# Rotary attention and a dense mixture of experts in one kernel: the softmax sums' constant, the spread's engine, and the order of work in the boundary between the two parts

## The chip, the core and the metric

The kernel runs on one core of one Trainium2 chip. A core has five engines that run their own instruction streams and wait for each other through semaphores: TensorE (PE in the rows, with its weight loads as PEld), VectorE (DVE), ScalarE (ACT), GpSimd (POOL) and SyncE (SP, which here only issues DMAs). The metric is device microseconds of one execution; where several runs are shown, their median. Line numbers (L361) are those of the kernel before.

## The reference

```python
# q, k, v: (2 batches, 8 heads, 576 positions, 64); w1: (4, 512, 1024); w2: (4, 1024, 512)
q_rot, k_rot = rotate(q), rotate(k)                      # rotary embedding on halves of 32
scores = np.matmul(q_rot, k_rot.transpose(0, 1, 3, 2)) / np.sqrt(D)
scores = scores - np.max(scores, axis=-1, keepdims=True)
attn = np.exp(scores)
attn = attn / (np.sum(attn, axis=-1, keepdims=True) + 1e-09)
x = np.matmul(attn, v)                                   # then heads are joined: (1152 tokens, 512)
p = domain_probs / (domain_probs.sum(-1, keepdims=True) + 1e-09)
for e in range(4):
    out += p[:, e:e + 1] * (np.maximum(x @ w1[e], 0.0) @ w2[e])
```

All four experts work on all tokens. Everything is float32.

## The kernel before, in words

**Numbers.** A float32 product of large matrices is made of three matmuls on rounded operands: each operand x is split into a high part (a copy rounded by the engine that writes it) and a low part (x minus the high part). For the weights `split` does that (L139 on ScalarE for `wh`, L146 on POOL for `wl`); for the tokens the pairs write `xH` and `xL`.

**Stages.** Tokens come in two chunks: chunk 0 is the first 512 positions of batch 0, chunk 1 the rest. A *pair* is two heads of one batch; there are four pairs in each batch. First the four pairs of batch 0 run alone (up to about 100 us). Then the experts of chunk 0 start (`start_experts`, at the agenda's time `end`), and the four pairs of batch 1 run between their matmuls: the boundary of which this document speaks is where this begins. About 350 us into the span the experts of chunk 1 begin.

**A pair.** Its keys and queries are loaded, rotated (on POOL), transposed on TensorE (`tpk`, `tpq`), and kept as `kT`, `qT` and `qTt` (the last 64 positions). In batch 1 `turn_whole` makes five transposes and `keep_whole` copies the high halves on ScalarE (L293) and writes the low ones on VectorE (L295); `swap` then exchanges the halves of the keys by two DMAs on SP (`k2T`). A pair has nine units: scores on TensorE (`sc`), the maximum on VectorE (`mx`), the exponential on ScalarE (`e`), which also adds up its rows into one column of `total`; transposes of e (`pp`), rounded as `pt` and `ptX`, and values (`x`). After the ninth unit `inverse` adds 1e-9 to the nine sums and takes their reciprocal (both on VectorE, in place), and `spread` copies eight of them out to a 128x512 tile (`rep`), which TensorE turns so that `divide` can multiply by it. `tail_rows` does that for the ninth.

**Experts.** For chunk 0, expert e has eight steps of the first layer (`ph`, f = 0 to 7, twelve matmuls of 512 columns each, then `hH` on ScalarE and `hL` on VectorE) and eight of the second (`po`), whose results VectorE adds into `acc`.

**Weights.** They come in blocks of 128x1024, one SP DMA each into one of two raw buffers (`wr`); a block's raw buffer is free when POOL has written its `wl`. `wts.next` issues the load of the next block and splits the one loaded before; there are five places for split blocks.

**What sets the order.** Each engine runs its instructions in the order in which the program issues them. The order comes from an agenda: `plan.at(t, f)` puts a piece of code at a time t in units of a pair's unit or an expert's step, and `plan.run` calls them by t. `ALONE` and `BESIDE` hold the times of a unit's pieces, `NEXT_TURNS` those at which a pair of batch 1 is turned (the first entry for the first pair, whose times are relative to the start of its scores, the second for the others). `later` puts a piece into a queue of jobs, of which two are done at each expert's step.

Of the kernel before, what the change touches and what calls it, by code (L numbers as in the profile page):

```python
# [14 lines left out]
F32 = mybir.dt.float32  # L15
F32R = mybir.dt.float32r
AF = mybir.ActivationFunctionType
ALU = mybir.AluOpType
AX = mybir.AxisListType
# [31 lines left out]
]  # L51
FIRST_TURNS = dict(q0=(1.327, 1.45), q1=(2.3, 2.5), q_tails=(-0.037, 0.16), swap=1.4)
NEXT_TURNS = [
    dict(k=(-0.75, -0.74), q=(0.6, 0.601), swap=(0.07,)),
    dict(k=(0.03, 0.056), q=(0.975, 1.004), swap=(0.07,)),
]


# [1 line left out]
def kernel(  # L60
# [36 lines left out]
    def f32(ap):  # L97
        return ap.bitcast(F32)
# [50 lines left out]
    class Pair:  # L149
# [196 lines left out]
        def scores(self, u):  # L346
            nm = f"{self.nm}_{u}"
            if u == 0:
                self.total = self.pool.tile([P, U], F32, tag="total", name=f"total{self.nm}")
            a = 0 if u % 2 else ST  # L350
            kT, kT2 = (self.tr[x][:, :, a : a + S] for x in ("k", "k2"))
            if u < TAIL:
                j, r = divmod(u, NR)
                qs = self.tr["q"][:, j, r * P : (r + 1) * P]
                terms = [(qs, kT[:, j, :]), (qs, kT2[:, j, :])]
            else:
                terms = [(self.qTt[:, j * P : (j + 1) * P], kk[:, j, :]) for j in range(2) for kk in (kT, kT2)]
            sc = banks["s"].tile([P, 2, 512], F32, f"sc{nm}")
            for n, (lhsT, rhs) in enumerate(terms):
                for i in range(2):  # L360
                    nc.tensor.matmul(  # L361
                        sc[:, i, 0:HALF],
                        lhsT=lhsT,
                        rhs=rhs[:, i * HALF : (i + 1) * HALF],
                        start=(n == 0),
                        stop=(n == len(terms) - 1),
                    )
            self.sc[u] = sc
# [8 lines left out]
        def exp(self, u):  # L377

            if u % 2 == 0:
                self.e2 = apool.tile([P, 2 * S], F32, tag="e", name=f"e{self.nm}_{u}", bufs=NE)  # L380
            a = u % 2 * S
            e = self.e2[:, a : a + S]
            nc.scalar.activation(  # L383
                out=e.rearrange("p (i c) -> p i c", i=2),
                in_=self.sc.pop(u)[:, :, 0:HALF],
                func=AF.Exp,
                bias=self.mx.pop(u),
                accum_out=self.total[:, u : u + 1],
            )
            self.e[u] = e[:, ST:] if u % 2 else e[:, 0:SM]  # L390
            if self.b == 0 or u == TAIL:
                self.ex[u] = self.e2[:, SM + u % 2 * ST :][:, 0:ST]
            elif u % 2:
                self.ex[u] = self.e2[:, SM : SM + P]
# [88 lines left out]
            )  # L483

        def inverse(self):
            nc.vector.tensor_scalar_add(self.total, self.total, 1e-9)
            nc.vector.reciprocal(out=self.total, in_=self.total)

        def spread(self):
            self.rep = apool.tile([P, NR, 2, D], F32, tag="rep", name=f"rep{self.nm}")  # L490
            by_row = self.total[:, 0:TAIL].rearrange("p (j r) -> p r j", j=2)
            nc.vector.tensor_copy(self.rep, by_row.unsqueeze(3).to_broadcast([P, NR, 2, D]))

        def rows(self):

# [5 lines left out]

        def tail_rows(self):
            self.prt = xb[1][:, 0:P] if banks["x"].n > 1 else xb[0][:, 3 * P : 4 * P]
            nc.tensor.transpose(self.prt, self.total[:, TAIL:].to_broadcast([P, P]), ident)

        def keep_tail_rows(self):
            if self.whole is None:
# [75 lines left out]
    class Weights:  # L583


        def __init__(self):
            self.order = [
                (c, e, which, fb)
                for c in range(NCHUNK)
                for e in range(E)  # L590
                for which in ((0, 2, 1) if c and not e else (0, 1))
                for fb in range(NF // FB)
            ]
            self.sums, self.lows = {}, collections.deque()
            self.raw, self.got = {}, {}
            self.loaded = self.done = 0

        def load(self):
# [13 lines left out]
            self.raw[key] = raw, f  # L612
            self.loaded += 1

        def split(self):
            if self.done == len(self.order):
                return
            key = self.order[self.done]
# [6 lines left out]
                return  # L625
            wh = wpool.tile([P, FB * DM], F32R, tag="h", name="wh%d_%d_%d_%d" % key, bufs=NRING)
            wl = wpool.tile([P, FB * DM], F32R, tag="l", name="wl%d_%d_%d_%d" % key, bufs=NRING)
            split(nc.scalar, nc.gpsimd, raw, wh, wl)
            self.got[key] = [x.rearrange("p (a f) -> p a f", f=f) for x in (wh, wl)]

        def finish(self):
# [20 lines left out]
            else:  # L652
                self.first_sums = lambda: split(nc.scalar, nc.gpsimd, x, sh, sl)

        def next(self):
            self.load()
            self.split()

    class Moe:

# [17 lines left out]
        def expert(self, e):  # L678
# [7 lines left out]
            for f in range(NF):  # L686
# [9 lines left out]
                        op0=ALU.max, op1=ALU.subtract,  # L696
                    )
                hh.append((tH, tL))
                if f % FB == FB - 1:
                    wts.next()  # L700
                yield
            po = [self.pp.tile([P, 512], F32, tag="m", name=f"po{c}_{e}_{t}") for t in range(n // P)]
# [313 lines left out]
    def pools(name, **kw):  # L1016
# [14 lines left out]
    first = [  # L1031
        Pair(0, hp, (evens, odds)[hp % 2], dst(0, hp, 0, SM), dst(1, hp, SM, S)) for hp in range(NP)
    ]
    qTt = [x.tile([P, 2 * P], F32R, name="qTt") for x in (evens, odds)]
    for x in (*qTt, tail_keys):
        nc.gpsimd.memset(f32(x), 0.0)
# [163 lines left out]
        plan.at(end + last - NF + 0.2 + 0.6 * i, quarter_step)  # L1200
    for i in range(6):
        plan.at(end + last - 1.3 + 0.1 * i, quarter_step)
    for t in (-1, 1.5, 5.3):
        plan.at(end + t, later(wts.next))
    plan.run()
    attn.close()
# [57 lines left out]
```

## Time and profile before

| | |
|---|---|
| runs | 568.74, 568.53, 567.66 us; median 568.53 us |
| the profiled execution | 567.32 us, span from first to last instruction 565.5 us |
| granted TensorE clock in it | 1.000 of full speed |
| TensorE busy | 537.2 us (95%) |
| VectorE, ScalarE, POOL busy | 334.8 us (59%), 288.0 us (51%), 326.5 us (58%) |

The rows are read as follows. In a timeline, each row has the start in us from the span's first instruction, the duration, the engine, the line, the operation, the tiles it writes and reads, their shapes, a count of merged instructions, and in brackets how long the engine was idle before it and which instruction ended the wait. Matmuls overlap, so that two that follow each other start closer together than a duration. The chain of waits follows the last instruction of a stretch back through what released it.

### The profile page before, as it was taken

To read this page: it belongs to the slowest core of one execution; us is meant where nothing else is said; L and a number is where in the kernel's file an instruction comes from. 1 tells how busy PE (TensorE), PEld (TensorE's weight loads), DVE (VectorE), ACT (ScalarE), POOL (GpSimd) and SP (SyncE) were. 2 spreads that over 40 slices of the span, in tenths; PEclk is the share of its full clock that TensorE was granted. 3 is DMA by queue.
4 is the path that set the end of the run, shared out by engine and by line. 5 is a ranking of instruction groups with operands and counts; after the bars stand their busy time and mean duration, and the time that the engine had idled before them with its cause. 6 is when DMAs were issued, how large, how long until landed. Compare 5 with 4: busy or idle time off the path is not lost.

```text
span 565.5 us, 8634 instructions
## 1 busy us (share of the span) xinstructions
PE 537.2 (95%) x3189; PEld 468.5 (83%) x3189; DVE 334.8 (59%) x617; ACT 288.0 (51%) x593; POOL 326.5 (58%) x241
## 2 busy tenths in 40 slices
PE   4898998989999999999999999999999999999996
PEld 3787787778877888788878888988898899889985
DVE  5589888354375435644365436894676576747602
ACT  5688888565545554655446553453344234325300
POOL 7999955459615752476344389558554664565400
PEclk9999999999999999999999999999999999999999
DMA  5245033244216221531242123622232213223102
GB/s 153 68 127 131 20 71 99 71 144 136 74 41 184 75 75 38 147 135 54 75 125 88 45 74 117 217 79 62 87 110 77 76 39 115 80 66 113 37 1 93
DMA packets 48732, 51.17 MB, mean 90 GB/s; under 512 B 15538, under 2 KB 38322, under 8 KB 48690
## 3 DMA queue, kind: packets, MB, share of 16 engines
q1 hardware_dynamic: 47890, 49.87, 29.3%
q10 hardware_dynamic: 800, 0.75, 0.5%
q8 instruction: 25, 0.41, 0.3%
q14 instruction: 17, 0.14, 0.1%
HBM read 43.34 MB, written 2.36 MB: 81 GB/s over the span
## 4 chain that ended last, share of the span: by engine, by line
PE 69%; DVE 11%; ACT 9%; POOL 5%; issue 3%; DMA 2%; SPq 1%; ACTq 0%; DVEq 0%; POOLq 0%
PE po L969 6%; PE po L970 6%; PE po L968 6%; PE sc L361 5%; PE p L880 5%; PE p L882 5%; PE p L881 5%; PE ph L734 4%; PE ph L735 4%; PE ph L733 4%; PE po L710 4%; PE po L708 4%; PE po L709 3%; PE pp L401 3%; ACT e L383 3%
## 5 line engine op out<-in xcount | busy, mean ns | idle before, releaser
L146 POOL TENSOR_TENSOR wl<-wr,wh 128x1024 fp32r<-128x1024 f32 x64 | 154.3, 2415 | 142.6 <-ACT wh L139 142.6
L139 ACT ACTIVATE wh<-wr 128x1024 fp32r<-128x1024 f32 x64 | 67.2, 1052 | 25.0 <-issue 11.9
L372 DVE TENSOR_REDUCE mx<-sc 128x1 f32<-128x576 f32 x72 | 54.2, 753 | 33.4 <-PE sc L361 32.6
L146 POOL TENSOR_TENSOR sl<-sf,sh 128x1024 fp32r<-128x1024 f32 x16 | 38.5, 2407 | 43.2 <-ACT sh L139 43.2
L970 PE MATMUL po<-wh,hL 128*128 128x512 f32 x160 | 62.3, 389 | 0.0
L969 PE MATMUL po<-wl,hH 128*128 128x512 f32 x160 | 62.3, 389 | 0.0
L968 PE MATMUL po<-wh,hH 128*128 128x512 f32 x160 | 62.3, 389 | 0.0
L383 ACT ACTIVATE e<-sc,mx 128x576 f32<-128x576 f32 x72 | 53.3, 741 | 17.4 <-DVE mx L372 16.5
L708 PE MATMUL po<-wh,hH 128*128 128x512 f32 x128 | 51.5, 403 | 0.0
L733 PE MATMUL ph<-xH,wh 128*128 128x512 f32 x128 | 51.1, 400 | 0.3 <-DVE acc L743 0.3
L420 DVE TENSOR_TENSOR pt<-pp,pt 128x512 fp32r<-128x512 f32 x64 | 43.9, 687 | 12.6 <-ACT pt L416 11.9
L734 PE MATMUL ph<-xL,wh 128*128 128x512 f32 x128 | 50.2, 392 | 0.6 <-POOL xL L524 0.6
L416 ACT ACTIVATE pt<-pp 128x512 fp32r<-128x512 f32 x64 | 38.1, 596 | 24.1 <-PE x L470 17.4
L710 PE MATMUL po<-wh,hL 128*128 128x512 f32 x128 | 50.3, 393 | 0.0
L735 PE MATMUL ph<-xH,wl 128*128 128x512 f32 x128 | 50.2, 392 | 0.0
L709 PE MATMUL po<-wl,hH 128*128 128x512 f32 x128 | 50.0, 391 | 0.0
L401 PE MATMUL pp<-ident,e 128*128 128x128 f32 x288 | 45.4, 281 | 3.9 <-ACT e L383 2.2
L694 DVE SCALAR_TENSOR_TENSOR hL<-ph,hH 128x512 fp32r<-128x512 f32 x32 | 22.2, 692 | 42.9 <-ACT hH L693 42.8
L920 ACT ACTIVATE hH<-p 128x320 fp32r<-128x320 f32 x64 | 26.1, 435 | 38.4 <-DVE p L911 38.4
L139 ACT ACTIVATE sh<-sf 128x1024 fp32r<-128x1024 f32 x16 | 16.9, 1059 | 51.4 <-DVE sf L644 51.4
L401 PEld LDWEIGHTS pp<-ident,e 128*128 128x128 f32 x288 | 34.5, 144 | 10.4 <-ACT e L383 4.2
L644 DVE TENSOR_TENSOR sf<-wr 128x256 f32<-128x256 f32 x30 | 32.7, 1126 | 17.4 <-DMA wr<-in_moe_w_dram 17.4
(212 smaller groups left out, 1359.2 us busy)
## 6 DMA issues: line engine op xcount, KB each, us to landing
wr<-in_moe_w_dram SPq DMA_DIRECT2D x68, 512.0 KB, 3.5
k2T<-kT SPq DMA_DIRECT2D x14, 320.0 KB, 4.5
rawv<-in_v_dram SPq DMA_DIRECT2D x16, 128.0 KB, 3.4
out_dram<-acc SPq DMA_DIRECT2D x8, 256.0 KB, 2.8
rawk<-in_k_dram SPq DMA_DIRECT2D x7, 256.0 KB, 3.9
rawq<-in_q_dram SPq DMA_DIRECT2D x7, 256.0 KB, 3.0
rawv<-in_v_dram SPq DMA_DIRECT2D x16, 32.0 KB, 2.9
tabs<-in_rope_dram ACTq DMA_DIRECT2D x1, 320.0 KB, 3.4
```

What stands on the lines that cost most here:

```text
L139: nc.scalar.activation(out=hi, in_=src, func=AF.Copy)
L146: eng_l.tensor_tensor(out=lo, in0=src, in1=f32(hi), op=ALU.subtract)
L383: nc.scalar.activation(out=e.rearrange("p (i c) -> p i c", i=2), in_=self.sc.pop(u)[:, :, 0:HALF], func=AF.Exp, bias=self.mx.pop(u), accum ...
L401: nc.tensor.transpose(pp[:, c * P : (c + 1) * P], self.e[u][:, c * P : (c + 1) * P], ident)
L708: nc.tensor.matmul(po[t], lhsT=sH, rhs=wH, start=(f == 0), stop=False)
L710: nc.tensor.matmul(po[t], lhsT=sL, rhs=wH, start=False, stop=(f == NF - 1))
L733: nc.tensor.matmul(o, lhsT=wH[:, kt], rhs=xh, start=(kt == 0), stop=False)
L734: nc.tensor.matmul(o, lhsT=wH[:, kt], rhs=xl, start=False, stop=False)
L735: nc.tensor.matmul(o, lhsT=wL[:, kt], rhs=xh, start=False, stop=(kt == KT1 - 1))
L968: nc.tensor.matmul(po[t], lhsT=sH, rhs=wH, start=(f == 0), stop=False)
L969: nc.tensor.matmul(po[t], lhsT=sH, rhs=wL, start=False, stop=False)
L970: nc.tensor.matmul(po[t], lhsT=sL, rhs=wH, start=False, stop=(f == NF - 1))
```

## The change

Five things are changed.

1. The nine sums of a pair have a second column beside them, set once to 1e-9 (two tiles, one for the even pairs and batch 1, one for the odd pairs of batch 0). `inverse` adds the two columns by a tensor_reduce into a new tile `inv`, and takes the reciprocal there. Before, it was a tensor_scalar addition in place.
2. In batch 1, `spread` is an activation on ScalarE and no longer a copy on VectorE.
3. The third and fourth weight blocks of the first expert are no longer split by a job at `end - 1` and in step f = 1, but at `end - 5.5` and `end - 0.1`; their low parts on POOL are issued at `end - 0.15` and `end - 0.09`.
4. The first pair of batch 1 has its keys turned before `end` (and the exchange of halves issued there), its queries about half a unit earlier.
5. For the other pairs of batch 1 the queries are turned 0.3 units earlier.

```diff
 NEXT_TURNS = [
-    dict(k=(-0.75, -0.74), q=(0.6, 0.601), swap=(0.07,)),
-    dict(k=(0.03, 0.056), q=(0.975, 1.004), swap=(0.07,)),
+    dict(k=(-1.2, -1.19), q=(0.0, 0.001), swap=(-1.1,)),
+    dict(k=(0.03, 0.056), q=(0.7, 0.701), swap=(0.07,)),
 ]
...
             if u == 0:
-                self.total = self.pool.tile([P, U], F32, tag="total", name=f"total{self.nm}")
+                self.total = totals[self.pool is odds]
...
-                accum_out=self.total[:, u : u + 1],
+                accum_out=self.total[:, u, 0:1],
...
         def inverse(self):
-            nc.vector.tensor_scalar_add(self.total, self.total, 1e-9)
-            nc.vector.reciprocal(out=self.total, in_=self.total)
+            self.inv = apool.tile([P, U], F32, tag="inv", name=f"inv{self.nm}", bufs=2)
+            nc.vector.tensor_reduce(out=self.inv, in_=self.total, op=ALU.add, axis=AX.X)
+            nc.vector.reciprocal(out=self.inv, in_=self.inv)
 
         def spread(self):
             self.rep = apool.tile([P, NR, 2, D], F32, tag="rep", name=f"rep{self.nm}")
-            by_row = self.total[:, 0:TAIL].rearrange("p (j r) -> p r j", j=2)
-            nc.vector.tensor_copy(self.rep, by_row.unsqueeze(3).to_broadcast([P, NR, 2, D]))
+            by_row = self.inv[:, 0:TAIL].rearrange("p (j r) -> p r j", j=2).unsqueeze(3).to_broadcast([P, NR, 2, D])
+            if self.b:
+                nc.scalar.activation(out=self.rep, in_=by_row, func=AF.Copy)
+            else:
+                nc.vector.tensor_copy(self.rep, by_row)
...
-            split(nc.scalar, nc.gpsimd, raw, wh, wl)
+            nc.scalar.activation(out=wh, in_=raw, func=AF.Copy)
+            low = lambda: nc.gpsimd.tensor_tensor(out=wl, in0=raw, in1=f32(wh), op=ALU.subtract)
+            if defer:
+                self.deferred.append(low)
+            else:
+                low()
...
+        def finish_split(self):
+            self.deferred.pop(0)()
...
-                if f % FB == FB - 1:
+                if f % FB == FB - 1 and (e or f >= FB):
                     wts.next()
...
+    totals = [x.tile([P, U, 2], F32, name="total") for x in (evens, odds)]
+    for x in totals:
+        nc.gpsimd.memset(x[:, :, 1:2], 1e-9)
...
-    for t in (-1, 1.5, 5.3):
+    for t, u in ((-5.5, -0.15), (-0.1, -0.09)):
+        plan.at(end + t, lambda: wts.next(True))
+        plan.at(end + u, wts.finish_split)
+    for t in (1.5, 5.3):
         plan.at(end + t, later(wts.next))
```

What this does to the order is seen in three places. The first is ScalarE in the boundary, before (`wh_0_0_2` and `wh_0_0_3` are the third and fourth weight blocks' high parts, `xH` the last pair's tokens, `kT` the next pair's keys, `hH_0_0` and `hH_0_1` the first two steps of the experts):

```order
L476 ACTIVATE tmp_3_3_1463<-x_114 64x256
L546 ACTIVATE xH_74<-xt_3_1448 128x64
L521 ACTIVATE xH_73<-xf_3_1309 128x512
L693 ACTIVATE hH_0_0_1519<-ph_0_0_0_1506 128x512
L139 ACTIVATE wh_0_0_2_1525<-wr_0_0_2_1260 128x1024
L293 ACTIVATE kT_0_1535<-tpk_0_1529 64x512 x2
L293 ACTIVATE kT_0_1535<-tpk_0_1529 64x2x64 x2
L693 ACTIVATE hH_0_1_1557<-ph_0_1_0_1544 128x512
L139 ACTIVATE wh_0_0_3_1563<-wr_0_0_3_1523 128x1024
```

The same place in the changed kernel, whose line numbers are its own:

```order
L476 ACTIVATE tmp_3_3_1467<-x_114 64x256
L632 ACTIVATE wh_0_0_2_1472<-wr_0_0_2_1263 128x1024
L550 ACTIVATE xH_74<-xt_3_1452 128x64
L525 ACTIVATE xH_73<-xf_3_1312 128x512
L632 ACTIVATE wh_0_0_3_1500<-wr_0_0_3_1470 128x1024
L293 ACTIVATE kT_0_1510<-tpk_0_1503 64x512 x2
L293 ACTIVATE kT_0_1510<-tpk_0_1503 64x2x64 x2
L705 ACTIVATE hH_0_0_1550<-ph_0_0_0_1537 128x512
L705 ACTIVATE hH_0_1_1570<-ph_0_1_0_1557 128x512
```

The third block's rounding has moved in front of both xH, the fourth's in front of kT, and kT in front of the first hH. POOL's order is unchanged but for the two memsets at the start.

The second place is TensorE there: the end of the first step's twelve matmuls and the keys' transposes behind them, before (`xL_75` in the second row is the low part of the last pair's tokens where its chunk is read):

```order
L733 MATMUL ph_0_0_0_1506<-xH_73,wh_0_0_0_1247 128x512
L734 MATMUL ph_0_0_0_1506<-xL_75,wh_0_0_0_1247 128x512
L735 MATMUL ph_0_0_0_1506<-xH_73,wl_0_0_0_1248 128x512
L271 MATMUL tpk_0_1529<-ident,rotk_0_873 128x128 x5
L733 MATMUL ph_0_1_0_1544<-xH_73,wh_0_0_0_1247 128x512
```

In the changed kernel, the end of the attention of batch 0 and the start of the first step:

```order
L502 MATMUL pr_3_1475<-ident,rep_3_1465 128x128 x4
L535 MATMUL x_113<-at_3_8_1435,rawv_3_1067 64x64 x8
L535 MATMUL x_113<-tail_keys,rawv_3_1067 64x64 x2
L271 MATMUL tpk_0_1503<-ident,rotk_0_876 128x128 x5
L745 MATMUL ph_0_0_0_1537<-xH_73,wh_0_0_0_1250 128x512
L746 MATMUL ph_0_0_0_1537<-xL_75,wh_0_0_0_1250 128x512
```

The five transposes stand in front of the twelve matmuls and no longer behind them. The queries' transposes likewise stand behind the second step and no longer behind the third.

The third place is VectorE where the first pair of batch 1 ends, before:

```order
L486 TENSOR_SCALAR total_0_1648<-total_0_1648 128x9
L487 RECIPROCAL total_0_1648<-total_0_1648 128x9
L442 TENSOR_TENSOR ptX_0_6_1992<-x_113,ptX_0_6_1992 64x128 x2
L492 COPY rep_0_2076<-total_0_1648 128x512
L694 SCALAR_TENSOR_TENSOR hL_1_0_2092<-ph_1_0_0_2078,hH_1_0_2091 128x512
```

and in the changed kernel:

```order
L487 TENSOR_REDUCE inv_0_2072<-total 128x9
L488 RECIPROCAL inv_0_2072<-inv_0_2072 128x9
L442 TENSOR_TENSOR ptX_0_6_1995<-x_113,ptX_0_6_1995 64x128 x2
L706 SCALAR_TENSOR_TENSOR hL_1_0_2096<-ph_1_0_0_2082,hH_1_0_2095 128x512
L295 SCALAR_TENSOR_TENSOR kT_1_2105<-tpk_1_2099,kT_1_2105 64x512 x2
```

The copy has left VectorE; on ScalarE it stands between ptX and that hH.

## Rows read from the trace of the kernel before

**Rows 1.** The page, busy time and share of the span, TensorE and its weight loads.
```profile
PE 537.2 (95%) x3189; PEld 468.5 (83%) x3189; DVE 334.8 (59%) x617; ACT 288.0 (51%) x593; POOL 326.5 (58%) x241
```

**Rows 2.** Timeline, TensorE: instructions behind a stop, from 100 us on.
```profile
103.31 0.50 PE L734 MATMUL ph<-xL,wh 128*128 128x512 f32 x1 [0.64 <-POOL xL L524]
...
116.72 0.50 PE L361 MATMUL sc<-kT,qT 128*128 128x288 f32 x2 [0.61 <-DVE qTt L295]
...
121.30 0.66 PE L401 MATMUL pp<-ident,e 128*128 128x128 f32 x4 [1.08 <-ACT e L383]
...
165.50 0.39 PE L469 MATMUL x<-pt,vs 128*128 128x256 f32 x1 [1.13 <-DVE ptX L442]
...
226.26 0.50 PE L733 MATMUL ph<-xH,wh 128*128 128x512 f32 x1 [0.32 <-DVE acc L743]
...
373.18 0.42 PE L880 MATMUL p<-tH,sh 128*128 128x320 f32 x1 [0.56 <-DVE hL L922]
```

**Rows 3.** Chain of waits in the boundary: start, us on the chain, what.
```profile
104.05 0.55 PE tpk L271 x5
...
109.07 2.42 POOL wl L146
...
111.50 5.80 DMA wr<-in_moe_w_dram
...
117.39 1.06 ACT wh L139
118.45 0.49 ACT hH L693
...
119.66 0.68 DVE mx L372
```

**Rows 4.** Timeline, ScalarE in the boundary.
```profile
99.11 0.38 ACT L476 ACTIVATE tmp<-x 64x256 f32<-64x256 f32 x1 [1.48 <-PE x L472]
101.13 0.26 ACT L546 ACTIVATE xH<-xt 128x64 fp32r<-128x64 f32 x1 [1.64 <-DVE xt L541]
101.30 0.62 ACT L521 ACTIVATE xH<-xf 128x512 fp32r<-128x512 f32 x1
...
105.53 1.75 ACT L293 ACTIVATE kT<-tpk 64x512 fp32r<-64x512 f32 x4
```

**Rows 5.** Timeline, POOL in the boundary.
```profile
101.99 1.27 POOL L524 TENSOR_TENSOR xL<-xf,xH 128x512 fp32r<-128x512 f32 x1 [0.20 <-ACT xH L521]
105.71 2.40 POOL L146 TENSOR_TENSOR wl<-wr,wh 128x1024 fp32r<-128x1024 f32 x1 [2.45 <-ACT wh L139]
```

**Rows 6.** The page, DMA issues: queue, count, size, median us to landing.
```profile
wr<-in_moe_w_dram SPq DMA_DIRECT2D x68, 512.0 KB, 3.5
k2T<-kT SPq DMA_DIRECT2D x14, 320.0 KB, 4.5
```

**Rows 7.** Line L486 by itself: shortest, median and longest duration in ns.
```profile
L486 DVE TENSOR_SCALAR total<-total x8: 172/460/1735, 33.2 to 338.0; 128x9 f32<-128x9 f32 x8
```

**Rows 8.** Timelines of VectorE and POOL, at 47 and at 162 us.
```profile
47.40 0.17 DVE L129 TENSOR_REDUCE ptot<-probs 128x9 f32<-128x36 f32 x1
...
162.84 1.74 DVE L486 TENSOR_SCALAR total<-total 128x9 f32<-128x9 f32 x1 [0.64 <-ACT e L383]
...
46.23 1.41 POOL L199 TENSOR_TENSOR t1k<-rawk,tabs 128x576 f32<-128x576 f32 x1
...
162.16 2.38 POOL L146 TENSOR_TENSOR wl<-wr,wh 128x1024 fp32r<-128x1024 f32 x1 [6.68 <-ACT wh L139]
```

**Rows 9.** Timeline, ScalarE: two hH with the waits before them.
```profile
163.86 0.60 ACT L693 ACTIVATE hH<-ph 128x512 fp32r<-128x512 f32 x1 [0.61 <-PE ph L735]
...
320.76 0.60 ACT L693 ACTIVATE hH<-ph 128x512 fp32r<-128x512 f32 x1 [1.57 <-PE ph L735]
```

**Rows 10.** Timeline, VectorE before the seam at 373 us.
```profile
347.75 1.28 DVE L550 TENSOR_TENSOR xL<-whole,xH 128x64 fp32r<-128x64 f32 x1 [0.32 <-ACT xH L546]
348.95 1.37 DVE L524 TENSOR_TENSOR xL<-whole,xH 128x512 fp32r<-128x512 f32 x1
```

More of the change, by code (lines that the diff above doesn't have):

```diff
@@ L503, in tail_rows @@
             self.prt = xb[1][:, 0:P] if banks["x"].n > 1 else xb[0][:, 3 * P : 4 * P]
-            nc.tensor.transpose(self.prt, self.total[:, TAIL:].to_broadcast([P, P]), ident)
+            nc.tensor.transpose(self.prt, self.inv[:, TAIL:].to_broadcast([P, P]), ident)
         def keep_tail_rows(self):
@@ L594, in __init__ @@
             self.sums, self.lows = {}, collections.deque()
-            self.raw, self.got = {}, {}
+            self.raw, self.got, self.deferred = {}, {}, []
             self.loaded = self.done = 0
@@ L613, in load, with split @@
             self.loaded += 1
-        def split(self):
+        def split(self, defer=False):
             if self.done == len(self.order):
@@ L653, in sum, with next @@
                 self.first_sums = lambda: split(nc.scalar, nc.gpsimd, x, sh, sl)
-        def next(self):
+        def next(self, defer=False):
             self.load()
-            self.split()
+            self.split(defer)
+        def finish_split(self):
+            self.deferred.pop(0)()
     class Moe:
```

## The prediction

> **What bounds the kernel now.** I read the page's busy shares first: TensorE is busy 95% of the span, and no other engine comes near [rows 1]. Where one engine is that full, time can only be won where it stands still, so the next view was the timeline of TensorE, read for the idle time in brackets. From the end of the first attention stage (100 us) on there are few stops, and six of them matter here [rows 2]. Three lie in the boundary between attention and the experts: 0.64 us for the last low part of the tokens (POOL xL), 0.61 us for the turned queries of the second batch's first pair (DVE qTt), 1.08 us for the first exponential (ACT e). One of 1.13 us lies where that pair ends (DVE ptX), one of 0.32 us at 226 us, one of 0.56 us in the seam to the second half of the tokens (373 us). Then I followed the chain of waits back from the largest of the boundary [rows 3]: the e waits for mx (DVE, 119.66), that for an hL and an hH, those for a weight rounding on ScalarE (117.39), that for a load of 5.8 us issued at 111.50, and the load for its buffer, which POOL's wl of 109.07 gives back. So the 1.08 us comes from weight rounding that starts too late, while in the same boundary ScalarE sits idle for 1.48 us before 99.11 and 1.64 us before 101.13 [rows 4].
>
> **The change, part by part.**
>
> *Two blocks rounded earlier.* ScalarE's row for the third block's high half now stands behind tmp, which ends at 99.11 + 0.38 = 99.49. One rounding takes 1.06 us [rows 3], so it ends at 100.55. The next instruction, xH from xt, cannot start before 101.13, since VectorE's xt releases it [rows 4]: 0.58 us to spare, cost nothing. If that cover were gone, each microsecond would be one on the path, since POOL's xL and the waiting matmul follow. The fourth block's rounding stands behind the xH that ends at 101.30 + 0.62 = 101.92, and ends at 102.98. On POOL both low halves stay behind the xL that ends at 103.26 [rows 5], so the matmul that waits for xL isn't touched; they run at 103.3 to 105.7 and 105.7 to 108.1, where they now start at 105.71 [rows 5] and 109.07 [rows 3]. The load that waits for the second is issued at 108.1, 3.4 us before its 111.50. With its present 5.8 us it lands at 113.9, and its rounding ends at 115.0.
>
> *Keys and queries turned earlier.* The five transposes of the keys take 0.55 us of TensorE, now after the xL wait [rows 3]; moved in front of the first ph they fill that wait: 0.64 becomes 0.09, gain 0.55 us. ScalarE copies kT at 102.98 instead of 105.53 [rows 4]; VectorE's half, and SP's exchange of key halves behind it (4.5 us to land [rows 6]), move with it by some 2.5 us. The queries are transposed one block of twelve matmuls earlier and on ScalarE no longer stand behind a rounding that waits for a load. Two hH later (about 107.6) ScalarE and then VectorE need about 1.75 us each, as for kT [rows 4], so qTt is ready near 111. TensorE reaches the score at 116.72 - 0.61 - 0.55 = 115.56: the 0.61 us is gone.
>
> *The first exponential.* From 115.56 on ScalarE isn't held by the load (115.0), so it waits for TensorE's fifth ph alone. From that hH (118.45) to the waiting matmul (121.30) are 2.85 us [rows 2, 3], which makes 118.4. TensorE comes there after a score and a block of matmuls, 121.30 - 1.08 - 116.72 = 3.5 us after 115.56, at 119.06. So 0.65 us to spare, and the 1.08 us is gone too. Boundary: 0.55 + 0.61 + 1.08 = 2.24 us.
>
> *The constant by tensor_reduce.* The eight tensor_scalar of nine columns take between 172 and 1735 ns [rows 7]. The longest, at 162.84, ends with POOL's wl that began at 162.16 and took 2.38 [rows 8]: it was held by POOL. A tensor_reduce to nine columns from SBUF took 0.17 us at 47.40 while POOL was in an instruction of 1.41 us that began at 46.23 [rows 8], so it isn't held. Then the reciprocal and ptX come 1.74 - 0.17 = 1.57 us earlier, more than the 1.13 us that TensorE waits for ptX [rows 2]; gain 1.13 us. The other three of the second batch end ahead of waits for other engines: nothing. For the first four the bounds are 0 and four times the median's excess, 4 x (460 - 172) ns = 1.2 us [rows 7]; the chain there goes through scores and exponentials and not through L486, so I take 0.
> The Trainium skill (SBUF — State Buffer, section Who interferes with whom) says the same as these rows for this chip, that copy and tensor_scalar can be shut out by GpSimd for a whole instruction and tensor_reduce never; another page (VectorE: DVE Perf Modes, Rules for kernel authors) speaks against the change, calling tensor_reduce the slowest VectorE operation. By that the eight might cost a little more than tensor_scalar does alone; the rows show 0.17 against 172 ns, so the sum stays.
>
> *The spread on ScalarE.* Four activations of 128x512; the nearest row of that size from SBUF is 0.62 us [rows 4]. In the first pair it stands in front of an hH that now waits 0.61 us for TensorE [rows 9]; in the other three the instruction behind it waits longer than that. Its input is ready when ptX ends on ScalarE. So nothing on the path; without that cover 4 x 0.62 = 2.5 us at the most.
>
> *The later turn.* For the third and later pairs the queries' transposes move forward; by the order only the third pair's pass a ph, and there they stand in front of the matmul that waits 0.32 us for acc [rows 2]: 0.55 us of work fills it, gain 0.32 us. The two memsets at the start lie in POOL's wait for the first load.
>
> Sum: 2.24 + 1.13 + 0.32 = 3.69, say 3.7 us. The profiled execution took 567.32 us (span 565.5 us), so it would take 563.6 us. That execution is 1.2 us under the median of the three runs shown, 568.53 us; taken from the median the sum gives 564.8 us, which I predict.
>
> **Rivals.**
> 1. *The load stays the bound.* Two weight loads and the key exchange now start between 105.7 and 108.1, closer together than before, and the 5.8 us was already longer than a weight load's usual landing of 3.5 us [rows 6]. If it lands after 115.2 (7 us), each further microsecond stays a stop. For it: the crowding. Against it: 1.2 us of room. With the whole 1.08 us left: 565.9 us.
> 2. *The reduce is held by POOL as well.* One row only speaks against it, and its overlap lasted just to POOL's end. Then the 1.13 us stays: 566.0 us.
> 3. *The lead is given back at the seam of 373 us.* There TensorE waits for VectorE [rows 2], behind a chain through POOL and ScalarE that starts with the hH of 320.76 [rows 9]. If that chain ran by loads, it would not come earlier, the 0.56 us would grow, and nothing much is left: 568 us. Against it: that hH waits for TensorE itself, so the chain should move along.
> 4. *More in the first stage.* The 1.2 us bound in full: 563.6 us.
> 5. *Slower.* In that same seam VectorE's subtractions with both inputs in SBUF take 1.28 us for 64 columns and 1.37 us for 512 [rows 10], so the small one is held by POOL. The instructions arrive at other moments now; each new meeting with a wl costs up to 2.4 us [rows 5], and the chain has no room there. It decides from two further full holds on: 4.8 - 3.7 = 1.1 us slower, 569.6 us or more. For it: holds of this kind are in the trace. Against it: POOL and VectorE move together there, behind the same TensorE rows.
>
> **Chances.** The forecast 0.67, rival 1 0.13, rival 2 0.05, rival 3 0.06, rival 4 0.05, rival 5 0.04. The three runs spread over 1.1 us, so the forecast's own range is 564.8 give or take 1; with rivals 1, 2 and 4 it becomes 563.2 to 567.0 us, which leaves out rivals 3 and 5 and the ends. A difference under 0.2% (1.1 us) can't be told from none here. Faster: the forecast and rivals 1, 2 and 4, less some for chance, 0.87; within 0.2%: 0.09; slower: 0.04.
>
> **What would show it.** In the profile after, TensorE's timeline has no stop over 0.2 us between the first ph and the first pp behind it, and none before x from pt near 162 us; TENSOR_REDUCE inv takes under 0.25 us eight times; wh of the third block starts near 99.5 and xH from xt still near 101.1. The forecast is wrong if a wr landing still releases wh before the first e, if inv takes a microsecond anywhere, if the spread on ScalarE waits, or if the stop near 370 us grows by what was won before it.

## The result, and the profile of the changed kernel

The changed kernel takes 563.35 us, median of 5 runs (562.42 to 563.66); the kernel before, measured with it, 568.39 us (567.66 to 568.74). The ratio is 0.9911, with a 95% interval of 0.9896 to 0.9925: 5.0 us faster, where 3.7 were forecast from 568.53 us. The profiled execution took 563.07 us (span 561.3), that of before 567.32.

The page's busy shares, against [rows 1]:

```profile
PE 536.9 (96%) x3189; PEld 469.2 (84%) x3189; DVE 329.0 (59%) x613; ACT 290.5 (52%) x597; POOL 325.7 (58%) x243
```

TensorE does the same 537 us of work in a shorter span, so what changed is its idle time. The timeline of TensorE at the places of [rows 2] (start, us, engine, line, operation, tiles, and idle time before with its releaser):

```profile
100.89 0.77 PE L271 MATMUL tpk<-ident,rotk 128*128 128x128 f32 x5
...
104.11 0.50 PE L746 MATMUL ph<-xL,wh 128*128 128x512 f32 x1 [0.16 <-POOL xL L528]
...
116.38 0.30 PE L361 MATMUL sc<-kT,qT 128*128 128x288 f32 x1
...
119.68 0.38 PE L401 MATMUL pp<-ident,e 128*128 128x128 f32 x2
...
162.32 0.36 PE L469 MATMUL x<-pt,vs 128*128 128x256 f32 x1
...
167.67 0.32 PE L508 MATMUL x<-ident,inv 128*128 128x128 f32 x1 [0.20 <-DVE xf L480]
...
226.21 0.32 PE L508 MATMUL x<-ident,inv 128*128 128x128 f32 x1
...
368.93 0.41 PE L892 MATMUL p<-tH,sh 128*128 128x320 f32 x1 [0.57 <-DVE hL L934]
```

The stops before sc, pp and x from pt are gone; that for xL has shrunk to 0.16 us. The best measure is the same matmul's start in the two traces, after less before. It is +0.80 us at the matmul that waits for xL (104.11 against 103.31), -0.34 at sc, -1.62 at pp, -3.18 at x from pt, and -4.25 at the seam, where the stop itself is unchanged (0.57 against 0.56). Behind the seam nothing is won or lost. From 104 us on that makes 0.80 + 4.25 = 5.05 us. The 0.80 us lost ahead of 100 us isn't counted against the change: the last section shows where it arises.

ScalarE in the boundary, against [rows 4]:

```profile
100.17 1.04 ACT L632 ACTIVATE wh<-wr 128x1024 fp32r<-128x1024 f32 x1
101.91 0.26 ACT L550 ACTIVATE xH<-xt 128x64 fp32r<-128x64 f32 x1 [0.69 <-DVE xt L545]
...
102.59 1.04 ACT L632 ACTIVATE wh<-wr 128x1024 fp32r<-128x1024 f32 x1
103.66 1.76 ACT L293 ACTIVATE kT<-tpk 64x512 fp32r<-64x512 f32 x4
...
115.53 1.06 ACT L632 ACTIVATE wh<-wr 128x1024 fp32r<-128x1024 f32 x1 [1.07 <-DMA wr<-in_moe_w_dram]
...
118.67 0.74 ACT L383 ACTIVATE e<-sc,mx 128x576 f32<-128x576 f32 x1 [1.48 <-DVE mx L372]
```

The first early rounding ends 0.7 us before xH starts, and xH still waits for VectorE: free, as forecast. But the rounding at 115.53, the last of the three shown, still waits for its load. That is the first of the signs by which the prediction wanted to be called wrong (a landing of wr that releases wh before the first e), and here it came without a stop of TensorE. SyncE's queue, with the start and duration of each issue, shows how near that was (the last row merges the load issued at 108.80 with the next, issued at 115.19, so its 6.76 us is no landing time):

```profile
106.44 0.37 SPq L613 DMA_DIRECT2D wr<-in_moe_w_dram  x1
107.21 0.53 SPq L323 DMA_DIRECT2D k2T<-kT  x1
107.79 0.58 SPq L324 DMA_DIRECT2D k2T<-kT  x1
108.80 6.76 SPq L613 DMA_DIRECT2D wr<-in_moe_w_dram  x2
```

Two weight loads and the exchange of key halves go out within 2.4 us. The second load, issued at 108.80, lands when wh starts at 115.53: 6.7 us, not the 5.8 us of [rows 3]. The windows of the boundary (busy time of the engines, clock, DMA share, GB/s) show the crowding: a DMA share over 1 in the first, where before has 0.65 (0.98 in the second).

```profile
109.00:111.00 2.00, 2.00 (x11) 1.64 (x10) 0.94 (x3) 1.03 (x3) 0.00 (x0) 1.00 1.13 320
111.00:113.00 2.00, 2.00 (x11) 1.65 (x10) 1.61 (x4) 1.55 (x2) 0.24 (x1) 1.00 0.97 204
```

TensorE does not wait for this load. The lines of the sums by themselves (shortest, median and longest ns), against [rows 7]:

```profile
L487 DVE TENSOR_REDUCE inv<-total x8: 173/175/175, 33.8 to 334.2; 128x9 f32<-128x18 f32 x8
...
L488 DVE RECIPROCAL inv<-inv x8: 215/216/216, 34.0 to 334.4; 128x9 f32<-128x9 f32 x8
...
L494 ACT ACTIVATE rep<-inv x4: 612/630/631, 161.5 to 336.0; 128x512 f32<-128x512 f32 x4
```

All eight reduces take 173 to 175 ns: none is held. The four spreads cost ScalarE 0.63 us each, and nothing waits for them.

### The profile page after: what moved, and what is told of

It is laid out like the page before. It is cut to its first block, busy times and chain, and to the rows that moved or that the text cites. A ratio compares the mean times of both kernels' runs of the same rounds, so it can differ in the third digit from the quotient of the medians.

```text
span 561.3 us, 8643 instructions
## 1 busy us (share of the span) xinstructions
PE 536.9 (96%) x3189; PEld 469.2 (84%) x3189; DVE 329.0 (59%) x613; ACT 290.5 (52%) x597; POOL 325.7 (58%) x243
## 4 chain that ended last, share of the span: by engine, by line
PE 71%; DVE 12%; ACT 9%; POOL 3%; issue 2%; DMA 1%; SPq 1%; ACTq 0%; DVEq 0%; POOLq 0%
PE po L982 6%; PE po L980 6%; PE po L981 6%; PE sc L361 5%; PE p L894 5%; PE p L892 5%; PE p L893 5%; PE ph L746 4%; PE ph L747 4%; PE ph L745 4%; PE po L720 4%; PE po L722 4%; PE po L721 4%; PE pp L401 3%; ACT e L383 3%
```

## The experiments

Where times of TensorE are given, they are a matmul's start less the start of the same matmul in the trace of before (or of the changed kernel, where it says so), and the gain of a stretch is the change of that figure across it. Such a figure holds for one profiled execution, and not all in it belongs to the edit: in the boundary up to the first pp, where the reduce changes nothing, the first kernel below gains nothing and the second loses 0.4 us.

**The reduce alone** (before, with the sums' constant added by tensor_reduce):

```diff
-            nc.vector.tensor_scalar_add(self.total, self.total, 1e-9)
-            nc.vector.reciprocal(out=self.total, in_=self.total)
+            nc.vector.tensor_reduce(out=self.inv, in_=self.total, op=ALU.add, axis=AX.X)
+            nc.vector.reciprocal(out=self.inv, in_=self.inv)
```

> The kernel before with the sums' constant added by tensor_reduce alone (the spread stays a copy on VectorE). Theory A, a stop is worth the start-to-start time that TensorE loses there, more than the idle shown, since matmuls no longer overlap across it: the values behind the stop at 165.5 us come 1.4 to 1.5 us earlier, 1.3 us of it left at 175 us and at the end. Theory B, a stop is worth the idle shown: 1.13 us there and at the end. Rival C, the reduce does nothing by itself and the gain at 165 us in the changed kernel came from the spread leaving VectorE: less than 0.3 us. All: nothing in the boundary at 100 to 125 us, nothing in the seam at 340 to 373 us.

564.9 us, ratio 0.9937 (0.992 to 0.9955). The timelines of TensorE and of VectorE where the first pair ends:

```profile
163.35 0.36 PE L469 MATMUL x<-pt,vs 128*128 128x256 f32 x1
```

```profile
162.06 0.17 DVE L487 TENSOR_REDUCE inv<-total 128x9 f32<-128x18 f32 x1 [0.60 <-ACT e L383]
162.27 0.21 DVE L488 RECIPROCAL inv<-inv 128x9 f32<-128x9 f32 x1
```

x from pt has no wait any more. The step is 1.41 us, more than the 1.13 us of idle time in [rows 2], as theory A had it; 0.3 us is given back at 170 us in a new stop for xf, and half of that returns at 175 us. The seam, where nothing was expected, brings 0.31 us. From 66 us on: 1.93 us. Ahead of it this execution gained 0.63 us, where its second spread copy isn't held (0.41 us at 58.64, against 1.35 us at 58.81 in before). The median's difference is larger still (3.9 us).

**Reduce and spread** (the same, and batch 1's copy on ScalarE):

```diff
-            nc.vector.tensor_copy(self.rep, by_row.unsqueeze(3).to_broadcast([P, NR, 2, D]))
+            if self.b:
+                nc.scalar.activation(out=self.rep, in_=by_row, func=AF.Copy)
+            else:
+                nc.vector.tensor_copy(self.rep, by_row)
```

> The kernel before with tensor_reduce and with the spread of batch 1 on ScalarE. Theory A: as with the reduce alone up to 320 us, then 0.2 us more in the seam, since the copy that ended at 341.65 held POOL's tL of 341.33 (1.06 us there, 0.87 us without it); if the wait of sh before 359.5 us also came from the copy, 0.5 us more. Rival, the spread's place is free as forecast and the seam's gain in the changed kernel comes from the other parts: no difference from the reduce alone, to 0.1 us, at any place. Rival, ScalarE pays for it: some 0.6 us back at 162 to 170 us.

565.0 us, 0.9937 (0.9922 to 0.9953): the same time. The pair's end again gives 1.41 us, so ScalarE doesn't pay for the spread. The seam gives 0.51 us, 0.20 more than by the reduce alone, as theory A had it. There, before, VectorE's spread copy and POOL's low part run at the same time (POOL, then VectorE):

```profile
341.33 1.06 POOL L798 TENSOR_TENSOR tL<-wide,tH 128x320 fp32r<-128x320 f32 x1
```

```profile
340.01 1.64 DVE L492 COPY rep<-total 128x512 f32<-128x512 f32 x1
```

In this experiment POOL's same instruction, on the chain to the seam, is 0.19 us shorter:

```profile
340.98 0.87 POOL L803 TENSOR_TENSOR tL<-wide,tH 128x320 fp32r<-128x320 f32 x1
```

The hold works both ways: POOL's wl of 339.00, which ends at 341.38, holds the copy, and the copy's end holds POOL. The Trainium skill (SBUF — State Buffer, Who interferes with whom) says that whichever of the two issues first has the shared ports for its whole instruction; these rows agree.

**Early blocks and early turn** (before, with both moves in the boundary, nothing else):

```diff
-    for t in (-1, 1.5, 5.3):
+    for t, u in ((-5.5, -0.15), (-0.1, -0.09)):
+        plan.at(end + t, lambda: wts.next(True))
+        plan.at(end + u, wts.finish_split)
+    for t in (1.5, 5.3):
...
-    dict(k=(-0.75, -0.74), q=(0.6, 0.601), swap=(0.07,)),
+    dict(k=(-1.2, -1.19), q=(0.0, 0.001), swap=(-1.1,)),
```

> The kernel before with the two early weight blocks and the early turn of the first pair, nothing else. Theory A (price by start to start): TensorE's first score of batch 1 and the pp behind it come 1.1 and 2.4 us earlier than before, measured from the last values of batch 0, and 2.4 us is left at the end. Theory B (idle shown): 2.24 us. Rival: what is won here is given back at 165 us, where the ptX then waits as long behind POOL: the stop there stays at 1.1 us or grows, and less than 2 us are left. All: the stop of 0.56 us at 373 us stays as it is.

565.74 us, 0.9946 (0.9928 to 0.9964). From +1.71 us at 66 us to -0.71 at pp: 2.42 us in the boundary, the same as in the changed kernel, and it stays to the end (-0.81). Nothing is given back at the seam.

**The early blocks alone** (the first half of that diff):

> The kernel before with the two weight blocks rounded early, first pair turned as before. Theory A: the load that ended the chain at 121.3 us is issued 3 us earlier, so hH of the fifth step waits for TensorE; the stop before the first pp (1.08 us idle, 1.27 us start to start) goes, the xL stop stays (0.6 us), the qTt stop stays or shrinks: 1.3 us at 121 us and at the end, up to 2.1 us if qTt was late only because ScalarE waited for a load. Rival: the late keys, not the load, set the first exponential, and less than 0.5 us is won without the early turn.

566.65 us, 0.9971 (0.9952 to 0.9989): 1.6 us in the trace, 0.83 at sc and 0.73 at pp. ScalarE's rounding and TensorE's first pp:

```profile
117.06 1.06 ACT L628 ACTIVATE wh<-wr 128x1024 fp32r<-128x1024 f32 x1 [1.80 <-DMA wr<-in_moe_w_dram]
```

```profile
120.97 0.66 PE L401 MATMUL pp<-ident,e 128*128 128x128 f32 x4 [0.35 <-ACT e L383]
```

The load still ends last, and 0.35 us of the stop is left. SyncE's queue shows one reason:

```profile
109.41 0.53 SPq L323 DMA_DIRECT2D k2T<-kT  x1
109.98 0.58 SPq L324 DMA_DIRECT2D k2T<-kT  x1
110.67 0.88 SPq L609 DMA_DIRECT2D wr<-in_moe_w_dram  x1
```

The load's buffer is free when POOL's wl ends at 109.20, but with the keys turned late the exchange stands in front of the load on SyncE, so it goes out at 110.67, right behind the exchange, and lands after 6.3 us.

**The early turn alone** (the second half):

> The kernel before with the early turn of the first pair alone. Theory A: the five transposes fill the xL stop (0.5 us) and qTt is in time (0.8 us), so the first score comes 1.1 to 1.3 us earlier, but wh still waits for the load issued at 111.5 us, and the stop before the first pp grows by nearly that much: 0.1 to 0.5 us at 121 us and at the end. Rival, turn and blocks work independently: 1.1 us left.

566.09 us, 0.9955 (0.9937 to 0.9972). The expectation was wrong: with no early rounding at all the trace gains 2.63 us up to pp, as much as both moves together, and keeps 2.5. ScalarE's roundings, which now come in their old order behind the turned keys:

```profile
105.81 1.05 ACT L139 ACTIVATE wh<-wr 128x1024 fp32r<-128x1024 f32 x1
108.64 1.05 ACT L139 ACTIVATE wh<-wr 128x1024 fp32r<-128x1024 f32 x1
113.95 1.06 ACT L139 ACTIVATE wh<-wr 128x1024 fp32r<-128x1024 f32 x1 [1.96 <-DMA wr<-in_moe_w_dram]
115.78 1.06 ACT L139 ACTIVATE wh<-wr 128x1024 fp32r<-128x1024 f32 x1 [0.29 <-DMA wr<-in_moe_w_dram]
```

The exchange goes out first, at 106.70, and the loads behind it, so each has the DMA engines more to itself (share 0.88 and 0.77 in the windows that have 1.13 and 0.97 in the changed kernel). The load issued at 112.20 lands in 3.5 us, and the block that held the first e is rounded at 115.78, about as early as in the changed kernel (115.53). So the 5.8 us of [rows 3] was itself a price of the exchange, which before went out at 109.06, 2.4 us ahead of that load, and was in flight until 116.27; here it has landed by 113.01. Which part of the early turn does it (keys, queries or exchange) was not tried apart.

**The later turn alone:**

```diff
-    dict(k=(0.03, 0.056), q=(0.975, 1.004), swap=(0.07,)),
+    dict(k=(0.03, 0.056), q=(0.7, 0.701), swap=(0.07,)),
```

> The kernel before with the later pairs' queries turned 0.3 units earlier, nothing else. Theory A: 0.4 to 0.5 us between 223 and 238 us, none elsewhere: 568 us, which timing alone can't tell from before, so the place in the trace decides. Theory B: 0.32 us. Rival: hL of the first step now stands behind the queries on VectorE and the exponential after it comes later, so the stop of 0.52 us at 237.8 us grows by what was won: 0.

568.13 us, 0.9988 (0.9974 to 1.0001). In the trace the gain is 0.32 us at 230 us and 0.46 us at 240 us, and it is kept; by time alone it can't be told from nothing.

**The changed kernel with both roundings in front of xH:**

```diff
-    for t, u in ((-5.5, -0.15), (-0.1, -0.09)):
+    for t, u in ((-5.5, -0.15), (-5.4, -0.09)):
```

> The changed kernel with the fourth block's rounding in front of xH too, directly behind the third's. Theory: the cover behind tmp (0.7 us of ScalarE idle in the changed kernel's trace) holds one rounding and not two; xH from xt starts about 0.35 us later, xL and the matmul that waits for it 0.3 to 0.5 us, and the stop of 0.16 us at xL grows to 0.5 to 0.7 us; the end is 0.3 to 0.5 us later than the changed kernel's in the trace from 100 us on. Rival: POOL, not ScalarE, sets xL, and nothing changes.

563.71 us, 0.9924 (0.9901 to 0.9946). Against the changed kernel the matmul that waits for xL loses 0.13 us and the next block wins 0.17 back: no loss there, against the expectation. The loss, 0.66 us, comes at pp, by the load: issued at 109.45, it lands at 116.81, after 7.4 us instead of 6.7. (This trace runs 0.5 us behind the changed kernel's from 66 us on, so the issue itself is only 0.15 us later.) ScalarE, then TensorE:

```profile
116.89 1.06 ACT L632 ACTIVATE wh<-wr 128x1024 fp32r<-128x1024 f32 x1 [1.97 <-DMA wr<-in_moe_w_dram]
```

```profile
120.80 0.66 PE L401 MATMUL pp<-ident,e 128*128 128x128 f32 x4 [0.50 <-ACT e L383]
```

So wh at 115.53 lies within its room and at 116.89 it is a stop of 0.50 us. Of the 1.36 us between the two, 0.46 is this trace's lag at that place: some 0.4 us of room was left behind the landing of the changed kernel. The forecast's landing of 113.9 is 114.7 on that trace's scale, so 0.75 us of the room was used up at 115.45: together the 1.2 us that rival 1 was given.

**The changed kernel with tensor_scalar in place of the reduce**, on the new tiles:

```diff
-            nc.vector.tensor_reduce(out=self.inv, in_=self.total, op=ALU.add, axis=AX.X)
+            nc.vector.tensor_scalar_add(self.inv, self.total[:, :, 0], 1e-9)
```

> The changed kernel with the constant added by tensor_scalar again, from the first column of the same tiles into inv. Theory A: at the first pair's end (159 to 162 us in the changed kernel) POOL writes a wl in the same place, so the addition is held for one to two us, and the values wait 1.1 to 1.5 us again: 1.3 us worse than the changed kernel. The wait of sh in the seam (0.3 us, gone in all kernels with the reduce) tells two things apart: if it comes back, the instruction brought it, if it stays away, the new tiles and their places did. Rival: the earlier weight blocks have moved POOL's wl away from that place, and the addition takes 0.2 us: no difference from the changed kernel.

563.84 us, 0.9924 (0.99 to 0.9948). Against the changed kernel 1.38 us are lost at x from pt and 0.19 more at 168 us: in the changed kernel's trace the reduce is worth 1.5 us. The seam keeps its gain, with sh as early behind sf as with the reduce. The line by itself, and TensorE's stop, which is back:

```profile
L487 DVE TENSOR_SCALAR inv<-total x8: 173/448/1742, 33.3 to 335.0; 128x9 f32<-128x9 f32 x8
```

```profile
162.89 0.38 PE L469 MATMUL x<-pt,vs 128*128 128x256 f32 x1 [1.14 <-DVE ptX L442]
```

**The changed kernel without the early blocks** (reduce, spread and both turns stay):

```diff
-    for t, u in ((-5.5, -0.15), (-0.1, -0.09)):
-        plan.at(end + t, lambda: wts.next(True))
-        plan.at(end + u, wts.finish_split)
-    for t in (1.5, 5.3):
+    for t in (-1, 1.5, 5.3):
```

> The changed kernel without the early rounding of two weight blocks: those are rounded as before, and the reduce, the spread, the early turn and the later turns stay. Theory C, formed after the turn alone had gained 2.5 us in the boundary and both together 2.4: the early rounding brings nothing once the keys are turned early, since its load is issued into the key exchange and lands after 6.7 us, where without it the load is issued later and lands after 3.5 us. Then the trace from 100 us on is 5.0 us shorter than before's, as the changed kernel's (5.05). Forecast's theory: the stop before the first pp comes back, 1 us worse than the changed kernel.

563.04 us, 0.9918 (0.9901 to 0.9935). Up to the first pp the trace is that of the changed kernel. Then 0.53 us are lost at the second pp (123.39 us) and 0.18 at 131 us, for ScalarE waits for the load after it:

```profile
113.93 1.06 ACT L139 ACTIVATE wh<-wr 128x1024 fp32r<-128x1024 f32 x1 [2.33 <-DMA wr<-in_moe_w_dram]
115.48 1.06 ACT L139 ACTIVATE wh<-wr 128x1024 fp32r<-128x1024 f32 x1
121.36 1.06 ACT L139 ACTIVATE wh<-wr 128x1024 fp32r<-128x1024 f32 x1 [1.03 <-DMA wr<-in_moe_w_dram]
```

Both theories missed: the early rounding isn't what frees the first e, and it isn't worth nothing. It saves 0.6 us one unit later, which the medians (563.04 and 563.35) don't resolve.

**The changed kernel with the key exchange issued behind the next load:**

```diff
-    dict(k=(-1.2, -1.19), q=(0.0, 0.001), swap=(-1.1,)),
+    dict(k=(-1.2, -1.19), q=(0.0, 0.001), swap=(0.45,)),
```

> The changed kernel with the key exchange of the first pair issued behind the sixth block's load and no longer in front of it. Theory C (DMA engines are full there): the load issued at 108.8 us in the changed kernel, which landed after 6.7 us, then lands after at most 4.5 us, so its rounding starts by 113.5 us and waits for no load, while the exchange lands near 115 us, just before the score at 116.4 us: no change for TensorE up to there, and 0 to 0.2 us earlier at the first pp. Rival: the landing is as long as before, and what delays it is the load in front of it or the memory.

561.6 us, 0.9894 (0.9875 to 0.9913), the lowest median. Yet from 66 us on TensorE keeps a constant distance to the changed kernel (-0.79 us there, -0.73 at the end): the boundary is no faster. The load lands at 114.28, 6.2 us after it was issued near 108.1, 0.5 us sooner than the 6.7, not the 2 us of theory C: what costs here is that load and exchange run at the same time, more than which goes first. The difference arises ahead of 66 us, where the kernels are alike.

**Batch 0's spread as a reduce over one element**, in the changed kernel, and in the one without the early blocks:

```diff
-                nc.vector.tensor_copy(self.rep, by_row)
+                nc.vector.tensor_reduce(out=self.rep, in_=by_row.unsqueeze(4), op=ALU.add, axis=AX.X)
```

> The changed kernel with the spread copies of batch 0 written as a tensor_reduce over one element, which POOL should not hold. Theory: the four take some 0.6 us each (512 elements at one a cycle, an estimate from mx's 0.75 us for 576), where the copies take 409 to 1224 ns; the held one at 59 us gets 0.6 us shorter, the free ones 0.2 us longer; TensorE at 66 us stands 0 to 0.4 us earlier against its place at 30 us. From 100 us on nothing changes. Rival: with a stride of zero it runs at half that speed or is held too, and the first stage gets longer.

> The same, with the spread of batch 0 as a tensor_reduce over one element. Theory: as the one without early rounding from 100 us on, and 0 to 0.4 us less before; by times about 563 us, which can't be told from it. Rival: a slower spread, 0.5 us more.

562.25 us, 0.9902 (0.988 to 0.9924), and 562.03 us, 0.9905 (0.9886 to 0.9925). The line by itself in the changed kernel, then in the first of the two:

```profile
L496 DVE COPY rep<-inv x4: 409/530/1224, 38.3 to 98.1; 128x512 f32<-128x512 f32 x4
```

```profile
L496 DVE TENSOR_REDUCE rep<-inv x4: 667/668/669, 38.7 to 98.1; 128x512 f32<-128x512 f32 x4
```

The reduce takes 0.67 us all four times, as expected; the copy takes 0.41 alone and 1.22 when POOL holds it. The Trainium skill (VectorE: DVE Perf Modes, Rules for kernel authors) calls tensor_reduce the slowest VectorE operation; at this width the rows agree as long as the copy runs alone (0.67 against 0.41), and not where it is held. At 43 us both traces have won 0.3 us on the changed kernel; at 52 us the first has won 0.2 more, the second has lost as much. The intervals of these three kernels and of the changed kernel overlap, so none of them is shown to be faster; the reduced spread is the one with a reason in its trace.

## Why the prediction was right, and where its sum was short

**Right.** The places were right: three stops in the boundary, the pair's end, the later turn. The reduce isn't held, ScalarE carries the spread for nothing, and the seam gives nothing back (rivals 2, 3 and 5 did not come). Undone or done apart, the parts nearly add up in the traces: boundary 2.4 us, reduce and spread 1.8 to 1.9, later turn 0.5. In the medians they don't: 3.9 us for the reduce alone, 3.0 for both moves of the boundary and 0.7 for the later turn make 7.6, against 5.0 for the whole, and undoing the reduce there costs only 0.5 (intervals of about 1 us each way). Medians hold the first 66 us too, where executions differ by up to 2.3 us (last section), so the shares of the parts rest on one trace each.

**The size.** From 104 us on the gain is 5.05 us where the terms made 3.69; 1.36 are missing in them.
- Boundary (to 121 us): 2.42 for 2.24. Pair's end (164 to 175 us, with what is given back behind it): 1.20 for 1.13. Later turn (223 to 240 us): 0.48 for 0.32. Together 0.41 us. The term that was mis-sized is the price of a stop: the sum took the idle time that the timeline shows in brackets. Start to start, a stop that goes altogether gives more: the exponential's 1.08 us gave 1.28, qTt's 0.61 gave 0.83, and ptX's 1.13 gave 1.41 in every kernel with the reduce. The matmul behind a stop has also lost its overlap with the one before it (in a run of 512 columns they last 0.39 us and start 0.23 apart). A stop that only shrinks gives no more than the idle time taken off: from 1.08 to 0.35 us in the early blocks alone gave 0.73, and from 0.64 to 0.16 at xL in the changed kernel gave 0.48. Against this stand 0.15 us lost where the queries' transposes now start (107.61), and the 0.2 us given back behind the pair's end.
- The seam: 0.48 us for the 0 of the forecast. 0.20 of it is the spread copy that no longer holds POOL's tL, which the forecast never costed: it asked what the copy costs ScalarE, not whom it had held on VectorE. The other 0.3 shows at a rounding of the sums of weights. In before, VectorE's sf and ScalarE's sh that waits for it:

```profile
358.72 0.42 DVE L644 TENSOR_TENSOR sf<-wr,sf 128x256 f32<-128x256 f32 x1
```

```profile
359.53 1.06 ACT L139 ACTIVATE sh<-sf 128x1024 fp32r<-128x1024 f32 x1 [3.46 <-DVE sf L644]
```

and the same two in the changed kernel:

```profile
354.75 0.43 DVE L653 TENSOR_TENSOR sf<-wr,sf 128x256 f32<-128x256 f32 x1
```

```profile
355.27 1.06 ACT L139 ACTIVATE sh<-sf 128x1024 fp32r<-128x1024 f32 x1 [3.18 <-DVE sf L653]
```

From the end of sf (359.14) sh takes 0.39 us to start in before, and 0.09 us in the changed kernel (from 355.18). The short gap comes with the new tiles for the sums: it is 0.09 us in all nine kernels that have them, with the reduce and with tensor_scalar alike, and 0.37 to 0.39 us in the five that keep the old ones. The new tiles are not shown to be the cause: in these nine ScalarE's stream also has six semaphore instructions more (134 for 128). What sh waited for beside sf, no record names. That stays open.
- The last 0.47 us are steps of some 0.05 us each, outside these places and ahead of 350 us, at matmuls that wait for nothing. Over the same stretches the reduce alone gains 0.4 us too, and the two moves of the boundary without it 0.1, so most of it comes with the reduce or its tiles; how isn't known.

**The mechanism of the first exponential.** Its stop went, but not by the step that the prediction gave. That said the earlier rounding frees the buffer, the load comes 3.4 us sooner and lands in 5.8 us, with 1.2 us to spare. The load was issued 2.7 us sooner, 3.5 when the 0.80 us by which this trace runs behind is taken off, as forecast. But it took 6.7 us, since loads and exchange crowd: rival 1's mechanism, which used up two thirds of the 1.2 us of room. The 5.8 us itself was no fixed cost of the load: with the exchange well ahead, in the early turn alone, the same load takes 3.5 us, and the stop goes without any early rounding. The early rounding alone removes two thirds of it (0.35 of 1.08 us is left), and on top of the turn it pays at the second pp, which the prediction didn't look at. The two moves are mostly two ways to the same 2.4 us: 1.6 and 2.5 us alone, 2.4 together, and 0.6 lost from the whole when the rounding is undone. That this term of the sum held in full was partly luck.

**The first stage.** The forecast took 0 between bounds of 0 and 1.2 us; single traces there differ by more than that for a reason of their own (below), so its share, and with it rival 4, isn't settled.

## What to carry to other kernels

Price a stop by the starts of the matmuls around it, not by the idle time shown: here stops of 0.6 to 1.1 us that went altogether were worth 0.2 to 0.3 us more each. An instruction that another engine can hold is worth changing for one that it can't, wherever something waits for it, and one that leaves an engine may free the engine that it held. Before a load's landing time is put into a sum, look at what was in flight beside it. When two edits aim at one stop, undo each by itself: the one that gets the credit may not be needed, and may pay somewhere else.

## What the runs showed of the hardware that was not expected

TensorE's clock rises for good at 22 to 25 us, and not at the same place in each execution: the records show a granted clock of 1.00 from 22.48 us on in before, from 23.45 us in the changed kernel, and from 22.07 to 24.76 us in the others. TensorE's last short matmul before the four transposes near 22.4 us, and the first of these, in before and in the changed kernel:

```profile
22.14 0.42 PE L428 MATMUL x<-ident,e 128*64 128x128 f32 x1
22.35 0.34 PE L401 MATMUL pp<-ident,e 128*128 128x128 f32 x1
```

```profile
22.18 0.42 PE L428 MATMUL x<-ident,e 128*64 128x128 f32 x1
22.40 0.42 PE L401 MATMUL pp<-ident,e 128*128 128x128 f32 x1
```

Up to here they run alike; the four transposes then take 0.67 us in before, across the rise, and 1.06 us in the changed kernel, which is 0.49 us behind at 24.5 us. The 1.06 us is the time at the lower of the two levels (1.2 GHz): in the kernel with reduce and spread, whose records cover this stretch, the same four take 1.06 us at 22.34 at a granted clock of 0.50 (the number behind the five engines' busy times; 0.24 is the DMA share):

```profile
18.00:24.00 6.00, 5.20 (x23) 4.82 (x23) 3.13 (x5) 3.88 (x11) 5.67 (x7) 0.50 0.24 55
```

That half microsecond decides whom the next instructions meet: the first spread copy takes 0.41 us at 37.80 in before and 1.22 us at 38.29 in the changed kernel, and it is 1.25 us too at 38.42 in the kernel with the early blocks alone, whose sums are those of before. In the four executions that were not behind at 24.5 us it takes 0.41 us, in the eight others that have it as a copy 0.95 to 1.33. So a trace of this kernel is ahead or behind by up to 1.7 us at 66 us for reasons that the change under test has no part in. Those four executions (before, the reduce alone, tensor_scalar in the changed kernel, the exchange behind) stand between -0.63 and +0.06 us at 66 us, all ten others between +0.75 and +1.71. Gains were therefore counted from 66 or 104 us on, and medians of a few runs that differ by a microsecond are not told apart here.
